# Output projections of the next group moved from behind the first MLP2 product to directly behind MLP1, in groups 3 to 7 of a transformer block

## The chip, the cores and the metric

The kernel runs on one core of a Trainium2 chip. The metric is the device time of one execution in microseconds. Seven runs of the kernel before gave a median of 365.28 us (364.97 to 365.79). The profile is of one further execution, with its own time.

## The reference

One pre-norm block on 2048 tokens of width 576: sliding, dilated attention (32 heads of 18, window 8, dilation 2), then an MLP of width 4608. All inputs are bf16.

```python
h  = x + attention(layernorm(x) @ wqkv) @ wo      # 8 keys for each query, at distances 0, 2, ..., 14
y  = layernorm(h)
h2 = h + gelu(y @ w1 + b1) @ w2 + b2
```

The product `@ wo` is the output projection. The second layernorm is called LN2 here, the two products of the MLP are MLP1 and MLP2.

## The kernel before, in words

**Tiles and groups.** The 2048 tokens are 16 tiles of 128. After a first stage (QKV for all tiles), the main loop (`for k, g in enumerate(GROUPS)`, L985) takes eight groups of two tiles. This document counts groups from 1, so group 3 is k = 2. In each group, TensorE (PE) does MLP1 of the group's 256 tokens, then its MLP2. In between it does the output projections of the two tiles c and d of the *next* group, so that their residual, LN2 and transposes can run on the other engines while PE is still in MLP2. Attention of the groups after that runs on VectorE (DVE) all along. The engines' orders are written out by hand (`manual_schedule`, L755): what the program issues first for an engine comes first in its queue.

**MLP1 and the projections (L210 to L250, L437, L545).** Both run as "visits". A visit takes two or three pairs of PSUM banks. Each matmul uses 64 of the 128 contraction rows, the two halves of the array working side by side into the two banks of a pair; then a second phase swaps the halves. Between the two phases stands a marker, a nop on GpSimd's queue (L226). PSUM has four pairs, called by tags that the loop rotates as p, q, r and s. MLP1 has four visits, on (p, q), (r, s), (p, q) and (r, s, p), 324 matmuls in all; the projections of c and d have one visit, on two pairs, with 36. ScalarE (ACT) empties MLP1's banks by GELU into `h_all` (L560), 36 calls a group. The projections' banks, named pw, are read by DVE, which adds the residual (L461).

**MLP2 (L685).** From group 3 on (`mlp2_fast`) it is a Strassen-like scheme. Two times two blocks of hidden activations and weights are combined so that, over `rows` pairs of hidden tiles (8, 12, 12, 16, 18, 18 in groups 3 to 8), seven products do the work of eight. The rest of the hidden tiles is multiplied plainly (steps "11", "12", "21", "22"). All these matmuls, named po, use 128 rows (L667). Products share results: product 1 is accumulated in bank a and is also needed in bank b, as the start of product 6. So ScalarE copies a to b when product 1 is done (step "b", L739), then product 2 goes on in a. In the same way "d" copies product 6's bank to that of product 5, and "f" product 5's to that of product 3. The sums of activations that the products use come from DVE (`h_sums`, L644).

**The order around the change.** A list `steps` in `mlp2_fast` gives the order (L723 to L734). A tuple is a product with its range of rows, "wo" is the visit of projections, and "h" holds the residual and LN2 of c and d: per tile DVE's addition (L461), three ScalarE calls (L478 to L480) and a power on GpSimd (L481), then a refill of the residual's tile with the bias by DMA (L505), and behind these some of the `h_sums`. "e" takes over the two pairs of the projections for products 7 and 5, once DVE has read them. At "6" and "7" ScalarE scales the normalized rows (L486, L175) and SP stores them. At "in" SP reads them back transposed as hnT (L496), the input of the next group's MLP1. "exp" is the softmax's exponential, "rest", "o1" and "o0" are additions into the output. The projections read oT, which SP writes by transposing DMAs (L433) that are issued while the group's MLP1 runs.

**Where the pairs go before.** `mlp2_fast` gets the tags (p, q, r, s): a and f lie in pair q, b in p, the projections and after them products 7 and 5 in r and s.

Of the kernel before, what the change touches and what calls it, by code (L numbers as in the profile page):

```python
# [17 lines left out]
def kernel(  # L18
# [77 lines left out]
    def psum_pair(tag, name, dtype=F32):  # L96
        n = 512 if dtype == F32 else 1024
        return psum.tile([P, 2, n], dtype, tag=f"ps{tag}", name=name)
# [352 lines left out]
    def x_of(j):  # L451
        return x_all[:, j - j % 2, :]
# [216 lines left out]
    def product(n, bank, m0, m1):  # L669
        lhs, rhs = PRODUCTS[n]  # L670
        for m in range(m0, m1):
            mm(bank, lhs(m), rhs(m), n in (1, 7) and m == 0, m == m1 - 1)

    def plain(i, half, bank, rows):
        for m in range(rows, NM):
            for odd in range(2):
                mm(bank, h_block(odd, i, m, m + 1), w2_block(odd, half, m, m + 1), False, m == NM - 1 and odd == 1)
# [4 lines left out]
    def halves(ap):  # L682
        return ap.rearrange("p (g c) -> p g c", g=2)

    def mlp2_fast(g, rows, tags, wo, hooks):  # L685
        p, q, r, s = tags
        last = wo is None
        j0, j1 = g
        af = psum_pair(q, "po")
        a, f = (af[:, n, 0:HALF] for n in range(2))  # L690
        b, d = psum_pair(p, "po")[:, 0, 0:HALF], None
        o0, o1 = (late.tile([P, D], BF16, tag="o_sb", name="o_sb", bufs=2) for _ in range(2))
        flat = kv_ring[int(rows == NM)][:].rearrange("p w t d -> p (w t d)")
        rest = q_all[:, 13:16:2, :].bitcast(F32) if SR < rows < NM else halves(flat[:, W * 2 * D - 2 * D:W * 2 * D].bitcast(F32))
        bank = {1: a, 2: a, 3: f, 4: b, 6: b}

        def add(out, x, y):
            nc.vector.tensor_tensor(out=out, in0=x, in1=y, op=ALU.add)

        def out0(n0, n1):  # L700
            add(halves(o0[:])[:, n0:n1], af[:, n0:n1, 0:HALF], halves(x_of(j0))[:, n0:n1])
            nc.sync.dma_start(out=out3[:, j0, n0 * HALF:n1 * HALF], in_=o0[:, n0 * HALF:n1 * HALF])

        def out1():
            add(o1[:, 0:HALF], b, rest[:, 0])
            add(o1[:, HALF:D], bank[5], rest[:, 1])
            nc.sync.dma_start(out=out3[:, j1, :], in_=o1[:])

        def do_rest():
            add(rest, bank[7].unsqueeze(1).to_broadcast([P, 2, HALF]), halves(x_of(j1)))  # L710

        def take():
            bank[7], bank[5] = (psum_pair(tag, "po")[:, 0, 0:HALF] for tag in (r, s))

        lo, hi, all_ = (0, SR), (SR, rows), (0, rows)
        seed = {"b": (1, 6), "d": (6, 5), "f": (5, 3)}
        does = {
            "wo": lambda: wo((r, s)), "e": take, "rest": do_rest, "o1": out1,
            "o0": lambda: out0(int(last), 2), "lo": lambda: out0(0, 1),
            "11": lambda: plain(0, 0, a, rows), "12": lambda: plain(0, 1, f, rows),  # L720
            "21": lambda: plain(1, 0, b, rows), "22": lambda: plain(1, 1, bank[5], rows),
        }
        if SR < rows < NM:  # L723
            steps = [(1, all_), "b", "wo", "h", "e", (2, all_), "11", (6, lo), (7, lo), "6", "7", (6, hi), "d", (7, hi), "rest", "in",
                     (5, all_), "f", "exp", (4, all_), "21", "22", "o1", "4", (3, all_), "12", "o0", "3"]
        elif rows <= SR:
            steps = [(1, all_), "b", "wo", "h", "e", (2, all_), "11", (6, all_), "d", "6", "7", (7, all_), "rest", "in",
                     (5, all_), "f", "exp", (4, all_), "21", "22", "o1", "4", (3, all_), "12", "o0", "3"]
        elif not last:
            steps = [(1, lo), "wo", (1, hi), "b", "h", "e", (7, lo), (6, all_), "d", "6", "7", (2, all_), (7, hi), "rest", "in",  # L730
                     (5, all_), "f", (4, all_), "o1", (3, all_), "o0"]
        else:
            steps = ["e", (1, lo), (7, lo), (1, hi), "b", "h", (7, hi), "rest", (6, all_), "d", (2, all_), "lo",
                     (5, all_), "f", (4, all_), "o1", (3, all_), "o0"]  # L734
        for step in steps:
            if isinstance(step, tuple):
                product(step[0], bank[step[0]], *step[1])
            elif step in seed:
                nc.scalar.copy(out=bank[seed[step][1]], in_=bank[seed[step][0]])  # L739
            else:  # L740
                call([does[step]] if step in does else hooks.get(step, ()))
# [9 lines left out]
    def call(fns):  # L751
        for fn in fns:
            fn()

    with tc.manual_schedule(engines={ENG.PE, ENG.Activation, ENG.DVE, ENG.SP, ENG.Pool}):  # L755
# [200 lines left out]
        def mlp1_plan(p, q, r, s, end):  # L956
            return [[([2 * v + n], tag) for n, tag in enumerate(tags)] for v, tags in enumerate(((p, q), (r, s), (p, q), end))]

        def mlp1(grp, plan, ahead, between, late=None):
            for v, duos in enumerate(plan):  # L960
                call(ahead.get(v, ()))
                visit([mlp1_duo(grp, us, tag) for us, tag in duos], None, between.get(v, ()), late if v == 3 else None)
# [15 lines left out]
        def wo_visit(*duos, fill=False):  # L978
            visit([wo_duo(j, tag) for j, tag in duos], (lambda: [ahead[0]() for _ in range(2)]) if fill else None)

        ROWS = {2: 8, 3: 12, 4: 12, 5: 16, 6: NM, 7: NM}
        p, q, r, s = "ABDC"

        gelu_table()
        for k, g in enumerate(GROUPS):  # L985
            c, d = GROUPS[k + 1] if k + 1 < len(GROUPS) else (None, None)
            e, f = GROUPS[k + 2] if k + 2 < len(GROUPS) else (None, None)
# [26 lines left out]
            rows = ROWS[k]  # L1014
            home = k % 2
            x = {n: [] for n in ("h", "6", "7", "in", "exp", "4", "3")}
# [29 lines left out]
            wo = None  # L1046
            if c is not None:
# [8 lines left out]
                x["in"] = [c_(ln2_ins, c, d)] + x["in"]  # L1056
                wo = lambda tags: wo_visit((c, tags[0]), (d, tags[1]))
            mlp1(g, mlp1_plan(p, q, r, s, (r, s, p)), m1, mid)
            mlp2_fast(g, rows, (p, q, r, s), wo, x)
            p, q, r, s = r, s, p, q  # L1060


# [28 lines left out]
```

## Time and profile before

| | |
|---|---|
| median of 7 runs | 365.28 us (364.97 to 365.79) |
| the profiled execution: its time, its span | 365.23 us, 363.4 us |
| granted TensorE clock | 1.0 of full speed |
| busy: PE, DVE, ACT, POOL | 358.3, 300.7, 229.3, 39.4 us |
| one po matmul, 128 rows x 288 columns | 286 ns from start to end |
| one pw matmul, 64 rows x 288 columns | 283 ns |
| one GELU, 128x256 | 495 ns |
| one seed copy, 128x288 (L739) | 384 ns |
| one addition of a residual (L461) | 751 ns |
| oT by transposing DMA, issue to landing | 2.7 to 4.7 us, median 2.9 |
| stages of groups 3 to 8 begin with MLP2 at | 162.3, 199.3, 235.8, 272.3, 308.7, 344.5 us |

How to read it: "busy" of an engine is the time in which the profile has it at work. PE's matmuls are pipelined: the next begins before the one ahead has ended, so that a duration is longer than the distance between two starts. PE, DVE, ACT, POOL and SP are TensorE, VectorE, ScalarE, GpSimd and the engine that issues DMAs. Releasers of waits are inferred from semaphores. The chain that ended last goes back from the last instruction to what released it, step by step.

### The profile page before, as it was taken

The numbers are of one execution on the slowest core, as the hardware profiler recorded it, in microseconds if no ns is written. First come the engines' busy times: TensorE is split into PE (matmuls) and PEld (weight loads), VectorE is DVE, ScalarE is ACT, GpSimd is POOL, SyncE is SP. The second block draws the span as 40 slices with busy tenths as digits, with TensorE's granted clock in tenths as the row PEclk, the third lists the DMA queues.
The fourth block names the chain that finished last, engine by engine and source line by source line (L and its number), as shares of the span: only waits on it lengthen the run. The fifth ranks groups of instructions, "written<-read, shape, count | busy, mean of one in ns | idle before, by whom it ended". The sixth has DMA issues, their size and how long they took to land.

```text
span 363.4 us, 11427 instructions
## 1 busy us (share of the span) xinstructions
PE 358.3 (99%) x4895; PEld 290.1 (80%) x4895; DVE 300.7 (83%) x426; ACT 229.3 (63%) x507; POOL 39.4 (11%) x47
## 2 busy tenths in 40 slices
PE   8999999999999999999999999999999999999996
PEld 5677777888788877887788778877887788778874
DVE  5999999999999999999999899979998498720441
ACT  4779856799626763668556855685568656615630
POOL 2250004000120030103100211020101010100000
PEclk9999999999999999999999999999999999999999
DMA  7998889975445733730552146304630352030001
GB/s 233 310 246 253 226 254 236 339 248 74 147 89 111 215 112 87 142 49 34 137 106 71 35 121 118 74 32 97 126 74 33 74 102 56 3 89 19 2 2 33
DMA packets 61907, 43.70 MB, mean 120 GB/s; under 512 B 31888, under 2 KB 60176, under 8 KB 61856
## 3 DMA queue, kind: packets, MB, share of 16 engines
q1 hardware_dynamic: 59968, 41.13, 41.5%
q0 software_dynamic: 1728, 1.77, 4.7%
q8 instruction: 38, 0.62, 0.7%
q10 hardware_dynamic: 160, 0.07, 0.1%
q14 instruction: 13, 0.11, 0.1%
HBM read 21.10 MB, written 12.42 MB: 92 GB/s over the span
## 4 chain that ended last, share of the span: by engine, by line
PE 93%; DMA 3%; ACT 1%; SPq 1%; DVE 0%; issue 0%
PE pm L217 39%; PE po L667 25%; PE pq L217 13%; PE po L579 10%; PE pw L217 5%; DMA wq_sb<-in_A_wqkv_dram 1%; DMA xnT<-xd 1%; SPq L104 1%; PE xt_pt L182 1%; DMA x_all<-b_bc 1%; ACT hn L175 0%; ACT hn L479 0%; DVE h L461 0%; PE h_pt L182 0%; PE o_pt L182 0%; ACT hn L478 0%
## 5 line engine op out<-in xcount | busy, mean ns | idle before, releaser
L560 ACT ACTIVATE h_all<-pm,b_sb 128x256 f16<-128x256 f32 (+1 forms) x288 | 108.5, 497 | 74.4 <-PE pm L217 74.4
L217 PE MATMUL pm<-hnT,w_sb 64*128 64x256 bf16 x2304 | 143.0, 269 | 0.0
L217 PEld LDWEIGHTS <-w_sb 64*128 64x128 bf16 x2304 | 111.7, 94 | 15.0 <-issue 1.7
L667 PEld LDWEIGHTS <-h_all 128*128 128x128 f16 x528 | 50.8, 98 | 14.9 <-issue 2.5
L217 PE MATMUL pq<-wq_sb,xnT 64*128 64x288 bf16 x768 | 54.7, 283 | 0.5 <-DMA wq_sb<-in_A_wqkv_dram 0.5
L217 PEld LDWEIGHTS <-xnT 64*128 64x128 bf16 x864 | 41.7, 94 | 11.7 <-issue 0.7
L351 DVE TENSOR_TENSOR prod<-prod 128x2304 bf16<-128x2304 bf16 (+1 forms) x64 | 44.2, 691 | 2.1
L667 PE MATMUL po<-w2a_sb,h_all 128*128 128x288 bf16 (+1 forms) x302 | 42.0, 286 | 0.0
L397 DVE TENSOR_TENSOR prod<-kv_ring,probs 128x4608 bf16<-128x4608 bf16 x16 | 40.9, 2554 | 0.9 <-DMA kv_ring<-kv_dram 0.6
L345 DVE TENSOR_TENSOR prod<-kv_ring,q_all 128x4608 bf16<-128x4608 bf16 x16 | 40.8, 2550 | 0.4
L217 PE MATMUL pm<-hnT,w1h_sb 64*128 64x256 bf16 x288 | 39.2, 269 | 0.0
L403 DVE TENSOR_TENSOR prod<-prod 128x2304 bf16<-128x2304 bf16 (+1 forms) x32 | 33.8, 1056 | 1.0
L579 PEld LDWEIGHTS <-h_all 128*128 128x128 bf16 x288 | 27.9, 98 | 7.9 <-issue 0.9
L481 POOL TENSOR_TENSOR ln_rstd<-ln_var,mhalf 128x1 f32<-128x1 f32 x13 | 14.5, 1118 | 174.5 <-ACT ln_var L480 174.5
L667 PEld LDWEIGHTS <-kv_ring 128*128 128x128 f16 x240 | 23.5, 98 | 6.4 <-issue 0.5
L579 PE MATMUL po<-w2a_sb,h_all 128*128 128x288 bf16 x224 | 28.5, 286 | 0.0
L647 DVE TENSOR_TENSOR kv_ring<-h_all 128x1536 f16<-128x1536 f16 (+3 forms) x10 | 6.9, 686 | 17.4 <-ACT h_all L560 17.4
L667 PE MATMUL po<-w2b_sb,h_all 128*128 128x288 bf16 (+1 forms) x142 | 21.2, 286 | 0.0
L217 PE MATMUL pw<-wo_sb,oT 64*128 64x288 bf16 x256 | 19.5, 283 | 0.0
L162 POOL TENSOR_TENSOR ln_rstd<-ln_veps,mhalf 128x1 f32<-128x1 f32 (+2 forms) x14 | 13.3, 956 | 48.2 <-DVE ln_veps L156 31.9
L217 PEld LDWEIGHTS <-oT 64*128 64x128 bf16 x288 | 13.4, 94 | 4.9 <-issue 1.7
L739 ACT COPY po<-po 128x288 f32<-128x288 f32 x18 | 6.9, 384 | 16.3 <-PE po L667 13.0
(117 smaller groups left out, 384.0 us busy)
## 6 DMA issues: line engine op xcount, KB each, us to landing
w_sb<-in_B_w_dram SPq DMA_DIRECT2D x6, 768.0 KB, 5.9
kv_ring<-kv_dram SPq DMA_DIRECT2D x28, 144.0 KB, 2.5
w2a_sb<-in_B_w_dram SPq DMA_DIRECT2D x4, 1008.0 KB, 7.6
kv_dram<-kv_ring SPq DMA_DIRECT2D x13, 288.0 KB, 3.3
out_dram<-o_sb SPq DMA_DIRECT2D x15, 144.0 KB, 2.6
td<-q_all SPq DMA_DIRECT2D x14, 144.0 KB, 2.3
td<-hn SPq DMA_DIRECT2D x14, 144.0 KB, 1.8
x_all<-in_A_x_dram SPq DMA_DIRECT2D x12, 144.0 KB, 2.8
```

Of the source, the lines that this page charges most:

```text
L162: nc.gpsimd.tensor_tensor(out=rstd[:], in0=veps[:], in1=mhalf[:].to_broadcast([P, n]), op=ALU.pow)
L217: last = nc.tensor.matmul(duo["g"][r ^ swap][i], lhsT=lhsT, rhs=rhs, start=(swap == 0 and i == 0 and kt == 0), stop=(swap == 1 and kt == K ...
L345: nc.vector.tensor_tensor(out=prod[:], in0=k_ring[j % 2], in1=q_all[:, j, :].unsqueeze(1) .to_broadcast([P, W, D]), op=ALU.mult)
L351: nc.vector.tensor_tensor(out=prod[:, :, o * H:o * H + n], in0=prod[:, :, a * H:a * H + n], in1=prod[:, :, c * H:c * H + n], op=ALU.add)
L397: nc.vector.tensor_tensor(out=prod[:].rearrange("p w (d h) -> p w d h", h=H), in0=v_ring[j % 2].rearrange("p w (d h) -> p w d h", h=H), in ...
L403: nc.vector.tensor_tensor(out=prod[:, 0:n, :], in0=prod[:, 0:n, :], in1=prod[:, n:2 * n, :], op=ALU.add)
L481: nc.gpsimd.tensor_tensor(out=rstd[:], in0=var[:], in1=mhalf[:], op=ALU.pow)
L560: pace[0] = nc.scalar.activation(out=hT(grp)[:, f, 0:N], in_=ps[:, r, i * N:(i + 1) * N], func=ACT.Gelu_apprx_tanh, bias=b1_sb[:, f:f + 1] ...
L579: nc.tensor.matmul(banks[half], lhsT=hT(grp)[:, f, i * P:(i + 1) * P], rhs=w2_rows(f)[:, half * HALF:(half + 1) * HALF], start=(f == 0), s ...
L647: nc.vector.tensor_tensor(out=s_slot(t, m0, m1), in0=a, in1=b, op=alu)
L667: nc.tensor.matmul(bank, lhsT=l, rhs=r, start=start, stop=stop, skip_group_check=True)
L739: nc.scalar.copy(out=bank[seed[step][1]], in_=bank[seed[step][0]])
```

## The change

In groups 3 to 6, "wo" moves from behind product 1 and the copy "b" to the front of the steps. In group 7, where it stood between two parts of product 1, it moves to the front too, and product 1 is in one piece. The list of group 8, which has no projections to make, stays as it is. On ScalarE the order stays: GELUs, the copy "b", LN2's statistics.

The pairs are dealt out anew, so that the projections find empty ones directly behind MLP1: they (and then products 7 and 5) go into q and r, a and f into s, b stays in p. The rotation for the next group is changed to match.

```diff
@@ mlp2_fast
-        p, q, r, s = tags
         last = wo is None
+        q, p, r, s = tags
@@ steps
         if SR < rows < NM:
-            steps = [(1, all_), "b", "wo", "h", "e", (2, all_), "11", (6, lo), (7, lo), "6", "7", (6, hi), "d", (7, hi), "rest", "in",
+            steps = ["wo", (1, all_), "b", "h", "e", (2, all_), "11", (6, lo), (7, lo), "6", "7", (6, hi), "d", (7, hi), "rest", "in",
                      (5, all_), "f", "exp", (4, all_), "21", "22", "o1", "4", (3, all_), "12", "o0", "3"]
         elif rows <= SR:
-            steps = [(1, all_), "b", "wo", "h", "e", (2, all_), "11", (6, all_), "d", "6", "7", (7, all_), "rest", "in",
+            steps = ["wo", (1, all_), "b", "h", "e", (2, all_), "11", (6, all_), "d", "6", "7", (7, all_), "rest", "in",
                      (5, all_), "f", "exp", (4, all_), "21", "22", "o1", "4", (3, all_), "12", "o0", "3"]
         elif not last:
-            steps = [(1, lo), "wo", (1, hi), "b", "h", "e", (7, lo), (6, all_), "d", "6", "7", (2, all_), (7, hi), "rest", "in",
+            steps = ["wo", (1, all_), "b", "h", "e", (7, lo), (6, all_), "d", "6", "7", (2, all_), (7, hi), "rest", "in",
                      (5, all_), "f", (4, all_), "o1", (3, all_), "o0"]
@@ the loop over groups
-            mlp2_fast(g, rows, (p, q, r, s), wo, x)
-            p, q, r, s = r, s, p, q
+            mlp2_fast(g, rows, (s, p, q, r) if wo else (q, p, r, s), wo, x)
+            p, q, r, s = q, r, p, s
```

## The prediction

> **What bounds the kernel now.** I read the page first, for the engine that sets the end.
>
> ```profile
> PE 358.3 (99%) x4895; PEld 290.1 (80%) x4895; DVE 300.7 (83%) x426; ACT 229.3 (63%) x507; POOL 39.4 (11%) x47
> PE 93%; DMA 3%; ACT 1%; SPq 1%; DVE 0%; issue 0%
> ```
>
> TensorE is busy in 99% of the span and makes 93% of the chain that ended last. So time is won or lost only where TensorE itself does less, or waits. The waits of PE, with the longest each:
>
> ```profile
> PE busy L783 <- PEq L1075: 0.8, 1, 0.8
> PE pq L217 <- DMA wq_sb<-in_A_wqkv_dram: 0.5, 2, 0.3
> PE po L667 <- ACT po L739: 0.3, 1, 0.3
> ```
>
> The third is the only one in the groups that the change touches: PE once waits for a seed copy on ScalarE. No bubble of size is left in groups 3 to 7 (k = 2 to 6), so earlier arrivals from DVE, ACT or DMA can save that one wait at most. What remains is in the seams. The chain in order of time gives each stretch of PE:
>
> ```profile
> 124.63 2.20 PE pw L217 x36
> 126.84 17.75 PE po L579 x144
> 144.58 17.79 PE pm L217 x324
> 162.37 1.09 PE po L667 x8
> 163.46 2.31 PE pw L217 x36
> 165.77 15.79 PE po L667 x128
> 181.56 17.79 PE pm L217 x324
> 199.35 1.58 PE po L667 x12
> 200.93 2.31 PE pw L217 x36
> 203.24 14.81 PE po L667 x120
> ```
>
> Columns: start, length, line, matmuls. pm and pw (MLP1, output projection) run on 64-row tiles, po (MLP2) on 128 rows. Let a po matmul take p, and a change between the two forms s. 144p + s = 17.75 and 128p + s = 15.79 give **p = 0.1225 us and s = 0.11 us**; 8p + s = 1.09, 12p + s = 1.58 and 120p + s = 14.81 come out of the same two numbers. The first line is the test: in group 2 the projections already stand directly behind MLP1, and 36 matmuls take 2.20 there, 2.31 behind a po stretch. The difference is again 0.11.
>
> **What the Trainium skill says.** "TensorEngine Tiling (Array Packing)", Key Properties: "Changing tiling mode (not just tile) drains the TensorE". The trace agrees, at 0.11 us a change. "TensorE: Matmul & The Clock Gate", Step-by-step: a matmul's drain is hidden only by the matmul that follows it. The trace agrees: one po matmul reads 0.286 us from start to end, yet they follow every 0.1225; whoever waits for the last one pays the difference. "PSUM — Partial Sum Buffer", Engine vs sequencer instructions: ScalarE's queue is strict FIFO and matmuls complete in program order. So a seed copy on ScalarE stands behind all that was queued before it, and PE behind the copy cannot pass on to other products.
>
> **The change, part by part.**
>
> *Order on PE, removed.* Before, each of groups 3 to 7 runs pm, product 1, pw, other po, next pm: four changes of form. After, pm, pw, po, pm: two. Two are saved in each of five groups: 10 x 0.11 = **1.10 us removed**, all on PE and so on the path.
>
> *Order on PE, added.* Product 1 goes into bank a. ScalarE then copies a into b (the seed of product 6), and only after that may product 2 add to a. Before, the whole projection visit (2.31 us) stood between product 1 and product 2 and hid the copy. After, with steps "wo", (1, all), "b", "h", "e", (2, all), PE has nothing between them in groups 3 to 6; "h" and "e" issue no matmul. Product 2 waits for product 1's last matmul, the copy, and the restart. Durations of these from the trace (timelines of groups 4 and 6):
>
> ```profile
> 206.12 1.63 PE L667 MATMUL po<-q_all,kv_ring 128*128 128x288 f16 x12
> 207.79 0.38 ACT L739 COPY po<-po 128x288 f32<-128x288 f32 x1 [0.32 <-PE po L667]
> ...
> 282.78 0.41 PE L667 MATMUL po<-w2b_sb,h_all 128*128 128x288 f16 x2
> 283.03 0.39 ACT L739 COPY po<-po 128x288 f32<-128x288 f32 x1
> 283.47 1.63 PE L667 MATMUL po<-x_all,kv_ring 128*128 128x288 f16 x12 [0.28 <-ACT po L739]
> ```
>
> Product 6's last matmul starts at 206.12 + 11 x 0.1225 = 207.47, the copy at 207.79: 0.32 from last start to copy. The copy takes 0.38. From a copy's end to PE's next matmul: 283.47 - 283.42 = 0.05. Sum 0.75; without a wait the next matmul would start after 0.12. **Stall 0.63 us in each of groups 3 to 6, 2.52 us in all.** Bounds, as the trace has only one such wait on PE: below, 0.47, if the exposed end of the last matmul (0.286 - 0.1225 = 0.16) did not count; above, 0.80, with a restart or an ACT start slower by 0.17. I take 0.63.
>
> *Is ScalarE free for the copy?* Its last 12 GELUs, ahead of the copy in its queue, end 2.9 us after PE leaves MLP1 (group 3: 160.67 + 4.50 = 165.17 against 162.3). In the new order product 1 ends after 2.2 of projections, 0.11, and 8 to 16 matmuls: at its shortest (group 3) the copy can start at 162.2 + 2.2 + 0.11 + 7 x 0.1225 + 0.32 = 165.7. GELU is out of the way by 0.5 us or more. Were it not, the stall would grow.
>
> *LN2 behind the copy.* Queued behind the copy on ScalarE are LN2's statistics, scalings and, later, copy d. In group 4 they began at 203.58 (4.3 us after MLP1); after, they begin at the copy's end, 2.2 + 0.11 + 11 x 0.1225 + 0.32 + 0.38 = 4.36 us after MLP1. Zero change; the next MLP1 starts no earlier in groups 4 to 7, so hnT has as much cover as now; group 8 starts 0.22 earlier, and its last transpose, issued at 322.5, lands 2.8 later at 325.3, against 326.65. DVE reads pw about 1 us earlier (in group 4 it idled 0.97 before), which only lengthens slack.
>
> *Group 6 (k = 5).* Here the copy d was late behind LN2 on ScalarE: PE's last matmul before product 5 starts at 282.90 and the next at 283.47, not 283.03: 0.44 lost. After, LN2 on ScalarE is where it was (copy b ends at 272.15 + 2.2 + 0.11 + 15 x 0.1225 + 0.70 = 277.0, LN2 began at 277.05), but PE arrives 0.63 - 0.22 = 0.41 later. Product 6's last matmul moves from 282.41 to 282.82, and copy d lets PE go 0.75 later, at 283.57: only 0.10 after 283.47. So 0.31 of the old wait is absorbed: **-0.31 us**.
>
> *Group 7 (k = 6).* Product 1 is no longer split, and behind it comes product 7's first part, 12 matmuls = 1.47 us into another bank, before product 6 needs the seed: 0.75 is hidden. Only the saving of 0.22 counts. If that cover failed, 0.63 more.
>
> *Banks and queues.* Projections now write q (read out a visit earlier) and r (read out first in the last visit), a is s, b is p; the next group gets the same roles in the same order, so no bank is waited for: s's GELUs end 1.4 us after MLP1, product 1 starts after 2.3. Only PE's order changes: product 1 issues nothing on SP, DVE or POOL. The projections' two POOL marker nops pass no other POOL instruction. Cost 0. *oT needed earlier:* tile d's transpose is issued at 268.99 in group 6 and lands 2.9 later (median), at 271.9; after, its first use is at 272.15 + 0.6 = 272.75. Cover is 0.9 us (as in group 7, 305.38 issued, used at 309.2); a landing of 4.7, the slowest seen, would cost 0.9 in a group. I take 0.
>
> *Sum.* -1.10 + 2.52 - 0.31 = **+1.1 us**. Profiled execution: span 363.4 becomes 364.5; its time 365.23 becomes 366.3. The median of the runs is 0.05 above that execution: 366.4 us, +0.3%.
>
> **The rivals.** *A smaller stall, no measurable change.* If ScalarE's turnaround costs 0.45 instead of 0.63, the sum is -1.10 + 1.80 - 0.31 = +0.4: 365.7. For it: only one PE restart is seen, and matmul ends are modelled. Against: the 0.32 to ACT's start repeats in group 5 (244.28, after a last start of 243.96).
> *Faster: the seed copy does not hold PE.* Place: product 1 to product 2 in groups 3 to 6. Were the copy's time covered, the ten saved drains and group 6's old wait remain: -1.10 - 0.44 gives 363.7. It decides where the stall is under (1.10 + 0.31) / 4 = 0.35 a group, less than the copy's own 0.38. Against it: the order leaves no matmul in between, and the copy must see product 1 alone.
> *Slower still: oT late.* Transposes landing as slowly as 4.7 us in two groups add up to 1.8: 368.2. Against: their queue is quiet there.
>
> **How the numbers follow.** Forecast 0.66, smaller stall 0.20, faster 0.08, oT late 0.06. Predicted: 366.4. The bounds of the stall give 365.28 + 4 x 0.47 - 1.41 = 365.75 and 365.28 + 4 x 0.80 - 1.41 = 367.1; I reach down to 365.6, to take in most of the rival next to it, and up to 367.2. About 0.2% (0.73 us) is what a measurement can tell from no change: above 366.0 is slower. Slower 0.66 + 0.06 = 0.72, same 0.20, faster 0.08.
>
> **What would show it.** In the chain, pw directly behind pm at 2.20 in groups 3 to 7 (drain right); PE waiting for ACT po L739 five times, 0.3 to 0.5 us each as the profile counts it (stall right), in groups 3 to 6 behind product 1 and once more in group 6; MLP1 starting without a wait for hnT. I am wrong if PE shows no such wait, if pw waits for oT, or if the later groups take back what the seams lose.

## The result and the profile after

The kernel after takes 366.77 us in the median, the one before 365.21 in runs beside it. The ratio is 1.0042, with a 95% interval of 1.0032 to 1.0051. That is slower by 1.2 to 1.9 us; 366.4 was forecast, within 365.6 to 367.2. The profiled execution took 366.78 us, with a span of 365.0.

The page's row of engines and the waits of PE (in total, times, longest):

```profile
PE 357.8 (98%) x4895; PEld 291.5 (80%) x4895; DVE 300.5 (82%) x426; ACT 229.2 (63%) x507; POOL 41.7 (11%) x47
PE po L667 <- ACT po L739: 2.1, 4, 0.5
```

PE has the same work, and where it waited once for ScalarE, for 0.3 us, it now waits four times, for 2.1. The chain in order of time shows both halves of the change in group 3:

```profile
144.77 17.79 PE pm L217 x324
162.56 2.20 PE pw L217 x36
164.77 1.10 PE po L667 x8
165.91 0.04 issue
165.95 0.39 ACT po L739
166.34 0.04 issue
166.38 15.85 PE po L667 x128
```

pw stands directly behind pm and takes 2.20 us, no longer 2.31: the drain is gone. Then the chain leaves PE, which it did not do here before: copy b lies on it, between 8 and 128 matmuls. The timeline of group 4:

```profile
202.15 1.64 PE L667 MATMUL po<-w2a_sb,h_all 128*128 128x288 bf16 x12
203.87 0.38 ACT L739 COPY po<-po 128x288 f32<-128x288 f32 x1 [1.07 <-issue]
204.17 0.69 ACT L478 ACTIVATE hn<-h 128x576 bf16<-128x576 f32 x1
204.31 2.12 PE L667 MATMUL po<-w2a_sb,h_all 128*128 128x288 bf16 x16 [0.52 <-ACT po L739]
207.25 1.63 PE L667 MATMUL po<-q_all,kv_ring 128*128 128x288 f16 x12
208.91 0.38 ACT L739 COPY po<-po 128x288 f32<-128x288 f32 x1 [0.84 <-PE po L667]
```

Product 1's last matmul starts at 202.15 + 11 x 0.1225 = 203.50, copy b 0.37 later, product 2 at 204.31: about 0.8 from start to start, where 0.12, the pitch (the distance between two starts), is usual within a product. The last two lines are product 6 and copy d, 0.32 behind product 6's last start (207.25 + 1.35 = 208.60). "0.52" is only what the profile counts as idle, from the modelled end of a matmul; the loss against the pitch is 0.68 here, and 0.69 in group 3.

A stage from one group's first MLP1 matmul to the next group's (in group 8, to the last matmul), taken from the timelines, shows where the time went, without what runs differ by in the QKV stage:

| stage, us | group 3 | 4 | 5 | 6 | 7 | 8 |
|---|---|---|---|---|---|---|
| before | 36.98 | 36.49 | 36.49 | 36.44 | 35.75 | 33.40 |
| after | 37.45 | 36.95 | 36.95 | 36.60 | 35.54 | 33.40 |
| difference | +0.47 | +0.46 | +0.46 | +0.16 | -0.21 | 0 |
| forecast | +0.41 | +0.41 | +0.41 | +0.10 | -0.22 | 0 |

The sum is +1.34 us. The first MLP1 of group 3, up to which both kernels are the same program, began 0.19 later in the profiled execution after; over the profiled executions of all versions in this document it began between 144.06 and 145.51, so this is no effect of the change.

### The profile page after: what moved, and what is told of

Same layout as the page of the kernel before. It is cut to its first block, busy times and chain, and to the rows that moved or that the text cites. A ratio compares the mean times of both kernels' runs of the same rounds, so it can differ in the third digit from the quotient of the medians.

```text
span 365.0 us, 11427 instructions
## 1 busy us (share of the span) xinstructions
PE 357.8 (98%) x4895; PEld 291.5 (80%) x4895; DVE 300.5 (82%) x426; ACT 229.2 (63%) x507; POOL 41.7 (11%) x47
## 4 chain that ended last, share of the span: by engine, by line
PE 77%; DVE 11%; DMA 5%; ACT 3%; issue 2%; SPq 1%; DVEq 0%; ACTq 0%
PE pm L217 29%; PE po L667 23%; PE pq L217 11%; PE po L579 10%; PE pw L217 3%; DVE prod L403 2%; DMA xnT<-xd 2%; DVE prod L397 2%; ACT h_all L560 2%; DVE prod L351 2%; DVE prod L345 1%; DMA wq_sb<-in_A_wqkv_dram 1%; DMA xd<-q_all 1%; SPq L104 1%; DVE o_sb L698 1%
## 5 line engine op out<-in xcount | busy, mean ns | idle before, releaser
L217 PEld LDWEIGHTS <-xnT 64*128 64x128 bf16 x864 | 42.5, 94 | 11.3 <-DMA xnT<-xd 0.8
L481 POOL TENSOR_TENSOR ln_rstd<-ln_var,mhalf 128x1 f32<-128x1 f32 x13 | 16.9, 1301 | 173.0 <-ACT ln_var L480 173.0
L508 POOL DMA_DIRECT2D x_all<-h x12 | 10.9, 1060 | 55.5 <-DMA hnT<-td 18.2
```

The lines of the kernel that those rows point to most:

```text
L217: last = nc.tensor.matmul(duo["g"][r ^ swap][i], lhsT=lhsT, rhs=rhs, start=(swap == 0 and i == 0 and kt == 0), stop=(swap == 1 and kt == K ...
L481: nc.gpsimd.tensor_tensor(out=rstd[:], in0=var[:], in1=mhalf[:], op=ALU.pow)
L508: ins = nc.gpsimd.dma_start(out=x_of(j), in_=h_of.pop(j)[:], accum_op=ALU.add).ins
```

## The experiments

The theory: two drains saved in each of five groups, and in groups 3 to 6 a wait of PE for copy b that the projections had hidden. The rival: the loss sits elsewhere, in pairs, oT or later groups.

**The copy b left out, in both kernels.** Product 6 then starts its bank afresh; one of the four results lacks product 1.

```diff
-            mm(bank, lhs(m), rhs(m), n in (1, 7) and m == 0, m == m1 - 1)
+            mm(bank, lhs(m), rhs(m), n in (1, 6, 7) and m == 0, m == m1 - 1)
-        seed = {"b": (1, 6), "d": (6, 5), "f": (5, 3)}
+        seed = {"d": (6, 5), "f": (5, 3)}
```

> The kernel after, with the seed copy b left out in groups 3 to 8: product 6 starts its bank afresh, so product 1 is missing from one of the four results; all matmuls stay. Theory (PE waits for copy b behind product 1, four times 0.68 us): no wait of PE for ACT is left in groups 3 to 5 and only the one of copy d in group 6; against before (365.2) ten drains of 0.11 are saved and about 0.3 of group 6's old wait, so 363.8 us, 3.0 below after. Rival (the loss comes from elsewhere, oT, pairs or the later groups): the time stays within 0.5 of after's 366.8.

> Control: the kernel before, with the same copy b left out in groups 3 to 8 (product 1 is missing from one result). Theory: the 2.3 us of projections hid the copy, so nothing changes: 365.2 us, within 0.2. Rival (the copy costs time on ScalarE or in PSUM wherever it stands): below 364.7, and then the gain of the run without b from the kernel after is not that of a wait alone.

Measured: 363.88 us without b from the kernel after (ratio to before 0.9963, 0.9949 to 0.9976), and 365.20 from the kernel before (0.9994, 0.9984 to 1.0003). The control's stages are those of before to 0.01 us. From the kernel after, they are 36.76, 36.27, 36.27, 35.92 and 35.54 in groups 3 to 7. Against after, each of groups 3 to 6 is 0.68 to 0.69 shorter: the price of the stall. Against before, they are 0.22 shorter in groups 3 to 5: the two drains. The chain without b, from the kernel after:

```profile
162.19 2.21 PE pw L217 x36
164.40 16.77 PE po L667 x136
181.16 17.79 PE pm L217 x324
198.95 2.21 PE pw L217 x36
201.16 16.27 PE po L667 x132
```

Products 1 and 2 have closed up into one stretch of 136 matmuls: 136 x 0.1225 + 0.11 = 16.77. The rival falls; the same copy is free in one order and costs 0.68 us in the other.

**Group 7 alone in the new order.**

```diff
-        p, q, r, s = tags
+        q, p, r, s = tags
...
-            steps = [(1, lo), "wo", (1, hi), "b", "h", "e", (7, lo), (6, all_), "d", "6", "7", (2, all_), (7, hi), "rest", "in",
+            steps = ["wo", (1, all_), "b", "h", "e", (7, lo), (6, all_), "d", "6", "7", (2, all_), (7, hi), "rest", "in",
...
-            mlp2_fast(g, rows, (p, q, r, s), wo, x)
-            p, q, r, s = r, s, p, q
+            mlp2_fast(g, rows, (s, p, q, r) if k == 6 else (q, p, r, s), wo, x)
+            p, q, r, s = (q, r, p, s) if k == 6 else (r, s, p, q)
```

> The kernel before with the new order and pairs in group 7 alone, where product 7 stands between product 1 and the need for the seed. Theory: two drains saved, no stall: group 7's stage 0.22 us shorter in the trace, 365.0 us. Rival (the drain saved in one seam turns up in the next, or group 8 waits for hnT): 365.2 and a stage as long as before.

Measured: 365.13 us, ratio 1.0006 (0.9992 to 1.0020). A time cannot show so little; the trace can. Group 7's stage is 35.54 against 35.75, the stages of all other groups are as before:

```profile
308.56 2.21 PE pw L217 x36
310.76 15.54 PE po L667 x126
326.31 17.79 PE pm L217 x324
```

All 126 po matmuls, the copy b somewhere inside, run without a gap: 12 matmuls of product 7 hide it.

**The copy behind LN2's statistics.**

```diff
-            steps = ["wo", (1, all_), "b", "h", "e", (2, all_), "11", (6, all_), "d", "6", "7", (7, all_), "rest", "in",
+            steps = ["wo", (1, all_), "h", "b", "e", (2, all_), "11", (6, all_), "d", "6", "7", (7, all_), "rest", "in",
```

The same exchange is made in the list of group 6.

> The kernel after with the copy b behind LN2's six statistics calls on ScalarE in groups 3 to 6 (steps h, b for b, h). Theory (ScalarE's queue is in order and PE stands behind the copy): the copy waits for DVE's residual and 3.9 us of statistics, PE restarts later by about 4.6, 3.2, 2.6 and 3.2 us in groups 3 to 6, so 380 us. Rival (the place of the copy in ScalarE's queue hardly matters, since the copy's wait for product 1 ends about when the statistics start): within 1 us of after's 366.8.

Measured: 385.43 us in two executions (1.0553, 1.0533 to 1.0573). The direction is that of the theory, the size is not: its stages are 6.01, 3.09, 4.28 and 5.95 us longer than after's, 19.3 in all, not 13.6. The timeline of group 3, and two stretches behind its wait (the first two numbers are the length and PE's busy time, the third from the end is the granted clock):

```profile
169.84 0.39 ACT L739 COPY po<-po 128x288 f32<-128x288 f32 x1
170.29 4.28 PE L667 MATMUL po<-w2a_sb,h_all 128*128 128x288 bf16 x20 [4.86 <-ACT po L739]
```

```profile
170.69:174.10 3.41, 3.41 (x17) 2.18 (x15) 3.31 (x4) 0.00 (x0) 1.38 (x1) 0.50 0.00 0
174.10:175.00 0.90, 0.90 (x9) 0.70 (x8) 0.83 (x3) 0.00 (x0) 0.00 (x0) 1.00 0.07 18
```

Twenty matmuls took 4.28 us behind the wait, where they take 2.61 in after: TensorE's clock had been taken back to a half. That lasted 3.41 us in groups 3 and 5 and 6.83 in group 6 (waits of 4.86, 3.13 and 3.81 us), and did not happen in group 4 (3.23 us). From start to start, the waits of groups 3 to 6 are 4.3, 2.7, 2.6 and 3.3 us longer than after's, 13.0 in all, near the 13.6 of the theory. What the theory did not foresee is the rest: about 1.7, 1.7 and 2.7 us at half clock in groups 3, 5 and 6, and 0.4 us in which the projections of group 4 waited for oT. The place of copy b on ScalarE, ahead of the statistics, is thus worth 19 us.

**Product 7 as cover in groups 4 to 6.** If the copy costs only because nothing stands behind product 1, the order can be mended. Group 3 keeps the old order, since its product 7 lacks a sum of weights until 165.98 in the timeline of after.

```diff
@@ groups 4 and 5
-            steps = ["wo", (1, all_), "b", "h", "e", (2, all_), "11", (6, all_), "d", "6", "7", (7, all_), "rest", "in",
+            steps = ["wo", (1, all_), "b", "h", "e", (7, all_), (2, all_), (6, all_), "d", "6", "7", "11", "rest", "in",
@@ group 6
-            steps = ["wo", (1, all_), "b", "h", "e", (2, all_), "11", (6, lo), (7, lo), "6", "7", (6, hi), "d", (7, hi), "rest", "in",
+            steps = ["wo", (1, all_), "b", "h", "e", (7, lo), (6, lo), (2, all_), "6", (6, hi), "d", "7", (7, hi), "11", "rest", "in",
@@ group 3: the old list, as in the kernel before; pairs by group (neither is printed here)
...
@@ group 4, DVE: the maximum behind the sums, product 7's sum early
-                m1[1] += [c_(att_qk_one, f, 1, home ^ 1), c_(att_max, (e, f))]
+                m1[1] += [c_(att_qk_one, f, 1, home ^ 1)] + ([c_(att_max, (e, f))] if k != 3 else [])
...
-                early = {2: (), 3: (0,)}.get(k, (0, 2))
+                early = {2: ()}.get(k, (0, 2))
+                if k == 3:
+                    x["h"] += [c_(att_max, (e, f))]
```

> The new order in groups 4 to 7 with product 7 (its first part in group 6) put between product 1 and product 2, steps 11 or product 7's rest behind copy d; group 3 in the old order with the old pairs; in group 4 one sum and the softmax maximum change places on DVE so that product 7 finds its operands. Theory (a stall of 0.68 is hidden by 12 matmuls of 0.1225 in another bank): four groups save 0.22 each and group 6 its old wait of 0.44, so 363.9 us, below both kernels, and PE waits for ACT by less than 0.2 in all. Rival (product 7 waits for its bank until DVE has read pw, or hnT comes late because ScalarE's sends are behind): a new wait of PE for DVE of 0.3 or more in each of groups 4 to 6, and 365.2 or more.

Measured: 365.20 us, ratio 1.0003 (0.9993 to 1.0013): the 1.3 us were not gained. Groups 4 and 5 did what was expected, with 36.27 each and no wait of PE for ACT. Group 6 took 37.18:

```profile
PE pm L217 <- DMA hnT<-td: 1.3, 1, 1.3
```

That is the rival's late hnT. LN2's second send stood behind copy d on ScalarE, but its last store was issued only 0.4 us later than in before (283.91 against 283.52); it landed 3.4 us after its issue (1.6 is the median), and the next MLP1 found no hnT. Two runs follow up. In one, both sends stand ahead of copy d ("6", "7", (6, hi), "d"); in the other, groups 3 and 6 keep the old order.

> As the run with all groups covered, but in group 6 both of LN2's sends stand ahead of copy d on ScalarE. Theory (there hnT was late by 1.3 us because the second send stood behind copy d, and one small store then landed late): hnT is in time, PE waits about 0.7 us for copy d, group 6's stage is as long as before (36.4), 364.6 us in all. Rival (the late landing of the store is not due to the place of the send): hnT is late again by a microsecond, a stage of 37 and 365.2 us.

> The cover of product 7 kept in groups 4 and 5, the kernel after's order in group 7, groups 3 and 6 as in the kernel before. Theory: three groups save their two drains, 3 x 0.22 = 0.66, and group 6 costs what it did before: 364.6 us, stages of groups 4, 5 and 7 at 36.27, 36.27 and 35.54 us, the rest as before. Rival (earlier MLP1 starts bring out a wait for hnT in group 6 or elsewhere, as in the run with all groups covered): 365.2.

Measured: 364.74 us (0.9996, 0.9976 to 1.0016) and 364.79 (0.9987, 0.9977 to 0.9997). With the sends ahead, the store lands in 1.6 us, hnT is in time and group 6 takes 36.37, with 0.4 us of waiting for copy d: behind LN2 on ScalarE, copy d sets this group's pace, and the shorter PE order brings nothing there. In the other run group 6 has its old order and takes 36.44, as before. That the place of the send made the store late is not shown: in the first of the three runs, while that store was under way, there ran a packet of 16 KB of another DMA queue, which the profile names "instruction" (285.02 to 286.21; the store's last piece ended at 286.38), and in the run with the sends ahead none did (the last section comes back to this). Two rows for the stretch 284.0 to 287.3 of the first:

```profile
q8 instruction: 1, 0.02, 2.3%
td<-hn SPq DMA_DIRECT2D x1, 16.0 KB, 3.4
```

The sums of the two later runs' stages are 0.6 and 0.5 us below before's. Only the second interval excludes no change, and barely: a gain of 0.1%. Group 4 gave 0.1 less than expected in both, 36.38:

```profile
200.89 1.46 PEld L217 LDWEIGHTS <-oT 64*128 64x128 bf16 x26 [0.24 <-DMA oT<-td]
```

This is from the run with groups 3 and 6 as before: oT's transpose was issued at 196.35 and landed 4.5 us later. That is no accident of this run. The transpose of group 4's tile d took 4.3 us in before, 4.5 in after, and 4.3 to 4.7 in all other traces but one, where it took 2.8. It is the prediction's rival "oT late", in small.

**Why copy b starts 0.37 and not 0.32 behind product 1.** All copies d and f that found ScalarE free begin 0.32 us after their product's last start, all copies b that wait for product 1 begin 0.37 after it. Ahead of these b, ScalarE's queue holds a wait as an instruction of its own; a copy d or f carries it itself. Two edits of the kernel after were to take that instruction away.

```diff
-        b, d = psum_pair(p, "po")[:, 0, 0:HALF], None
+        bd = psum_pair(p, "po")
+        b, d = bd[:, 0, 0:HALF], None
+        nc.scalar.copy(out=bd[:, 1, 0:1], in_=mhalf[:])
+        nc.scalar.copy(out=warm[:], in_=bd[:, 1, 0:1])
```

The first run has only the first of the two copies.

> The kernel after with one more, tiny call on ScalarE (one column, into the unused second bank of b's pair) behind the GELUs and ahead of copy b, so that it takes over those waits of copy b that have nothing to do with product 1. Theory (copy b starts 0.37 behind product 1's last matmul and not 0.32, because a separate wait instruction stands ahead of it in ScalarE's queue): with that gone, 0.32, and the stages of groups 3 to 6 are 0.04 to 0.05 shorter than after's (37.40, 36.90, 36.90, 36.55), 366.6 us. Rival (the 0.37 belongs to a matmul that no other follows, or to the bank): 0.37 as before, stages as after's, 366.8.

> As the run with the tiny call, and behind it a second one that reads what the first wrote, so that ScalarE has also waited for its own earlier calls before copy b comes; what is left for copy b to wait for is product 1 alone. Theory (the separate wait instruction costs the 0.05): copy b starts 0.32 behind product 1's last matmul, no wait instruction of its own ahead of it, and the stall in groups 3 to 6 is 0.05 shorter. Rival (it belongs to a matmul that no other follows): still 0.37, with no wait instruction there.

Measured: 367.33 us (1.0048, 1.0029 to 1.0067) and, in one execution, 367.34. No stage got shorter: groups 3 to 6 took 37.45, 37.06, 37.12 and 36.61 in the first. In both traces the separate wait for PE stayed where it was, and copy b began 0.38 behind product 1. So the edits did not make the case that was to be tested. The trace of after tells where the 0.05 lies, though: in group 4 the separate wait ended at 203.83, 0.33 behind product 1's last start, and copy b began 0.04 later. Product 1 is thus seen as early as copy d sees product 6, which speaks against the rival; that the time goes away with the instruction is not shown, since no run removed it. The second run also shows a wait of 1.2 us for hnT ahead of group 8, in that one execution; it was not followed up.

## Why the prediction was right

**The chain and PE's waits** were the right views: PE set the end, and what was decided was decided between stretches of PE.

**Ten drains saved, 1.10 us**: right. Without the copy, groups 3 to 5 are 0.22 shorter than before, and group 7 alone in the new order 0.21. "TensorEngine Tiling (Array Packing)", Key Properties, says that a change of mode drains the array; the pitch of 0.1225 and the two lengths of pw, 2.31 and 2.20, had given its price before any run.

**The stall, 2.52 us**: the mechanism was right, the size a little low. It measured 0.69 + 3 x 0.68 = 2.73. The mis-sized term is "0.32 from last start to copy", which came from copy d; copy b takes 0.37. The right row was in the profile of before: in groups 7 and 8 copy b itself waited for product 1, and began 0.37 behind its last matmul. The copy (0.38) and PE's restart (0.05) came out as forecast. The 0.286 us of one po matmul, which the prediction took as agreement with its drain, is a modelled end; what is measured is that the copies begin 0.32 or 0.37 behind a matmul's start, and not 0.12.

**ScalarE free for the copy, LN2 unmoved, pairs and queues at 0**: right. The GELUs were done, no PE wait for hnT, oT or a bank appears in after, and the statistics began as soon as the copy was over.

**Group 6, -0.31**: right. Without b, that stage is 0.52 below before, 0.22 of it drains, so 0.30 of the old wait. In after, PE reaches product 5 with 0.14 us lost at copy d, as the sum of 0.75 against five matmuls (0.61) says:

```profile
284.77 0.38 ACT L739 COPY po<-po 128x288 f32<-128x288 f32 x1
284.81 0.41 PE L667 MATMUL po<-w2b_sb,h_all 128*128 128x288 f16 x2
285.20 1.63 PE L667 MATMUL po<-x_all,kv_ring 128*128 128x288 f16 x12
```

The forecast named five waits for ACT; the profile counts four and puts this small one down to nothing.

**The rivals.** A stall of 0.45 and a stall that is covered both fell with the run without b. Late oT cost nothing in after, but it was close: I had measured its cover in groups 6 and 7 with the median landing, 0.9 us. In group 4 the transpose was issued at 195.87, landed 4.45 us later at 200.32, and its tile was loaded for the first matmul at 200.36. A landing of 4.3 us in that very group stood in the trace of before. That it cost nothing in this trace was luck: two versions with cover and the first one with the tiny call, whose order on PE is that of after, lost 0.1 us to it, and the one with the copy behind the statistics 0.4.

**The sum**: +1.1 forecast, +1.34 in the stages, of which four times 0.05 or 0.06 is the copy's later start. The ratio's interval, 1.2 to 1.9 us, holds the stages' sum; the forecast of 1.1 lies just below it, for the reason given.

## What to carry to other kernels

When a step is moved away from between two uses of one PSUM bank, look for what it was hiding: here 2.3 us of other matmuls had covered a bank copy of 0.38, which costs 0.68 once PE has to stand and wait. Price the whole turnaround (last start to copy, copy, restart, less one pitch), from the row of that very copy, and set it against the gain of the move: two drains of 0.11 do not pay for it. A dozen matmuls into another bank hide it fully, unless another engine's chain, as LN2's in group 6, then sets the end.

## What the runs showed of the hardware that was not expected

**Which waits halve the clock.** In the run with the copy behind the statistics, PE waits of 4.86, 3.13 and 3.81 us brought the granted clock to 0.50, and one of 3.23 us did not. The half-clock stretches begin at 170.69, 252.61 and 293.57 and last 3.41, 3.41 and 6.83 us; the distances between their beginnings, 81.92 and 40.96, are 24 and 12 times 3.413. In before, the one stretch at full clock lasts 358.40 us, 105 times as much, and it is a whole multiple in the other traces, too. So the clock changes on a grid of 3.41 us. Cut along this grid, the stretches around the waits of groups 3 to 6 read (length, PE's busy time; the granted clock is the third number from the end):

```profile
167.28:170.69 3.41, 0.40 (x4) 0.32 (x4) 3.39 (x4) 2.86 (x9) 1.43 (x2) 1.00 0.22 78
208.24:211.65 3.41, 1.50 (x12) 1.07 (x11) 3.41 (x5) 2.95 (x9) 0.63 (x1) 1.00 0.25 89
211.65:215.06 3.41, 2.09 (x18) 1.66 (x18) 3.38 (x3) 1.24 (x4) 2.07 (x1) 1.00 0.00 0
249.19:252.61 3.42, 0.29 (x3) 0.10 (x2) 3.39 (x3) 3.19 (x9) 0.92 (x2) 1.00 0.24 86
290.15:293.57 3.42, 0.98 (x8) 0.64 (x7) 3.35 (x6) 2.90 (x8) 0.76 (x1) 1.00 0.25 89
293.57:296.98 3.41, 2.05 (x9) 1.28 (x9) 2.54 (x7) 3.31 (x8) 0.55 (x1) 0.50 0.03 8
296.98:300.39 3.41, 3.41 (x16) 2.06 (x14) 0.00 (x0) 0.11 (x1) 0.00 (x0) 0.50 0.30 88
```

Ahead of each drop PE had idled 3.01, 3.13 and 2.44 us of one grid stretch. The wait of 3.23 us fell across a border of the grid, at 211.65, with 1.91 us on one side and 1.32 on the other, and the clock stayed. In this trace it was not the length of a wait that counted but how much of one grid stretch it filled: 2.44 us was enough, 1.91 was not, and nothing in between occurred. In group 6 the clock stayed at half for a second stretch, behind one in which PE was busy for 2.05 us only. "TensorE: Matmul & The Clock Gate", What's actually happening, speaks of an idle window of about 3.4 us that runs freely and so does not start with the wait. The grid agrees with that. A window that is idle throughout was not needed here, as the 2.44 us show; the measurement stands. The waits of about 0.5 us in after left the clock at 1.00.

**What a late DMA met.** The transposing DMA of group 4's tile d took 4.3 to 4.7 us to land in ten of the eleven traces and 2.8 in the other, where the median of its kind is 2.9. In the ten, a 16 KB packet of the queue named "instruction" began while it was under way; in the other, such a packet began only in the last 0.12 us before it landed. The small stores of LN2 and the attention (16 KB, second half of a send) show the same, counted over all traces from 170 us on: 99 of them met no packet of the two queues named "instruction" (16 and 8 KB a packet) between issue and landing and took 1.5 to 1.6 us; 66 met one and took 1.6 to 3.8. That the packet is the cause is not shown: the two coincide in the traces, other transfers ran at some of these times, and no run changed it. The prediction's "their queue is quiet there" speaks of the transposes' own queue; these packets came by another.
